# A Fourier-mixing and ELU kernel on one core: one gather for each backward tile instead of two, odd rows loaded in later steps, and scalar pairs in other steps

## Chip, cores and metric

The kernel runs on one core of one Trainium2 chip. The metric is the device time of one execution in microseconds (us). Given times are the median of the runs, with the lowest and highest; a profile comes from one execution of its own, whose time is given beside its span.

## What is computed

The reference takes `x` of shape 8 x 3008 x 256 in float32 and two weight matrices:

```
X = np.fft.fft(np.fft.fft(x, axis=1), axis=2).real      # 8 x 3008 x 256
h = X.reshape(24064, 256) @ w_in                         # w_in 256 x 2048
g = np.where(h > 0, h, np.exp(np.minimum(h, 0)) - 1)     # ELU
out = g @ w_out                                          # w_out 2048 x 256
```

## The kernel before, in words

**Main stream.** Only half of the frequencies along the sequence are computed; the other half follows by symmetry ("plus" and "minus" columns). The columns of all eight batches stand in rings in SBUF (`Rr`, `Ir`, `Rb`), and are worked through in 47 tiles of 256 columns. A tile has 8 slots, so there are 376 of them; a slot is called a step here. In each step TensorE (PE) does, in this order: `mm_P` (H from `Rr`), `mm_X1` of an earlier step (products of the second matrix), `mm_Q` (adds `Ir` to H), `mm_X2` and `mm_X3`. The second product is done with seven instead of eight block products (Winograd's scheme), which needs four sums of 128x256 blocks, `sum_1`, `sum_3`, `sum_2`, `sum_4`, on GpSimd (POOL). `mm_X1` uses the result of `sum_2` in its last product (the group pB<-G,WT). VectorE (DVE) has `even_part` (L1332, out E; it must have read H before `mm_Q` adds to it), `g_plus` and `g_minus` (L1362), `h_minus` (L1346). ScalarE (ACT) does the exponentials. At the end of each group of 8 steps DVE also combines and transposes a finished output tile (`comb_1`, `comb_2`, `comb_22`, `comb_3`, `turn_u`, `turn_v`), and SyncE (SP) issues the stores (L1563), 8 to 32 for each half of a tile.

**Side stream.** While the main stream works on one batch, the Fourier transform of the next is prepared in the gaps, for batches 2 to 7 by the "quarter" method. Four input tiles of up to 96 partitions with four rows of 256 values each are loaded by `load_quarter`, once for the near and once for the far part of the sequence. Two of the four tiles run forwards in memory and are loaded by SP (L337). The other two run backwards (j = 1, 2 in the near part, j = 0, 3 in the far part): two of their four rows come by an indirect DMA from POOL each (a gather, L303, with an index for each partition), the other two, called odd here, by SP with a negative step (L317, L326). Then POOL folds the tiles (`mirror_sum`, `channel_fold`), DVE adds halves (`half_sum`) and makes scalar pairs (`quarter_pairs` and `shift_pairs` with odd frequencies: two SCALAR_TENSOR_TENSOR of 94x128 in `turn`, L863), PE does small matmuls (QM), and DVE unfolds the result into the rings.

**What sets the order.** A list of events, each with a time in steps of `PERIOD` = 4.8, is sorted, and the functions are called in that order. Compute instructions and gathers are pinned to it on their engine (`pin`). DMAs of SP are not pinned: a scheduler places them in SP's queue, and each of them also waits for the transfer eight before it. For batch b the side stream's first step is r0 = 48b - 70 (`rel`). The near loads are events of steps 2 and 3 after r0, the far ones of steps 25 to 28, `mirror_sum` starts at steps 6 and 30, `shift_pairs` stands at steps 47 to 50, 54 and 55, always at the end of the step (4.25). `comb_1` and `comb_2` stand at 4.2 of every step that is 1 modulo 8, which steps 47 and 55 are.

Of the kernel before, what the change touches and what calls it, by code (L numbers as in the profile page):

```python
# [11 lines left out]
U32 = mybir.dt.uint32  # L12
# [5 lines left out]
SEQ = 3008  # L18
ND = 256
NDFF = 2048  # L20
NF = NDFF // 128
HALF = SEQ // 2
# [10 lines left out]
NP = 47  # L33
SHIFT = 8 * NP
# [141 lines left out]
def kernel(  # L176
# [7 lines left out]
    nc = tc.nc  # L184
    NB = x.shape[0]
# [20 lines left out]
    pin = tc.keep_in_program_order  # L206

    xt = x.tensor

    def xrows(b, row, step, n, rows=6):  # L210

        return bass.AP(
            tensor=xt,
            offset=x.offset + (b * SEQ + row) * ND,
            ap=[[step * ND, n], [1, rows * ND]],
        )


    xflat = x.rearrange("b s d -> (b s) d")
    ix = cpool.tile([128, 6], I32, tag="ix")  # L220
# [20 lines left out]
    def load_x(b):  # L241

        L = [
            spool.tile([128, 6 * ND], FP, tag=f"xl{j}", bufs=1, name=f"xl{j}")
# [3 lines left out]
        def back(j, few):  # L248
            cols = slice(0, 2 * ND) if few else slice(2 * ND, 6 * ND)
            c = 1 if few else 0  # L250
            pin(
                nc.gpsimd.indirect_dma_start(
                    out=L[j][:, cols],
                    out_offset=None,
                    in_=xflat,
                    in_offset=bass.IndirectOffsetOnAxis(
                        ap=ix[:, c : c + 1].bitcast(U32), axis=0
                    ),
                    element_offset=(b * SEQ + (HALF if j == 1 else 0)) * ND,
                )  # L260
            )
        def ahead(j, row):
            nc.sync.dma_start(out=L[j][:, 0 : 4 * ND], in_=xrows(b, row, 4, 128, 4))
            nc.sync.dma_start(
                out=L[j][:, 4 * ND :], in_=xrows(b, row + 512, 2, 128, 2)
            )

        loads = [lambda n=n: back(2 - n // 2, n % 2) for n in range(4)]
        return L, loads + [lambda: ahead(3, HALF), lambda: ahead(0, 0)]

# [18 lines left out]
    def load_quarter(b, j, far):  # L289

        L = spool.tile([128, 6 * ND], FP, tag=f"xl{j}", bufs=1, name=f"xq{j}")
        if j == 0:
            state["rest"] = L[:, 4 * ND :]
        state["L", j, far] = L = L[:, 0 : 4 * ND]
        rows = L.rearrange("p (m d) -> p m d", d=ND)
        back = j in (1, 2)
        base = b * SEQ + (0, SEQ, HALF, HALF)[j]
        if back != far:
            n = 94 if far else 96
            for i in (0, 2) if far else (3, 1):  # L300
                c = 3 if far else 5 if j == 1 and b == NB - 1 and i == 3 else 4
                pin(
                    nc.gpsimd.indirect_dma_start(  # L303
                        out=rows[0:n, i],
                        out_offset=None,
                        in_=xflat,
                        in_offset=bass.IndirectOffsetOnAxis(
                            ap=ix[0:n, c : c + 1].bitcast(U32), axis=0
                        ),
                        element_offset=(  # L310
                            b * SEQ + (HALF if j in (1, 3) else 0) + i
                        ) * ND,
                    )
                )
            row = base + (749 if far else -3)
            for i, shift in (((3, 0), (1, SHIFT)) if far else ((2, 0), (0, SHIFT))):
                nc.sync.dma_start(  # L317
                    out=rows[0 : 2 * NP, i],
                    in_=bass.AP(
                        tensor=xt,  # L320
                        offset=x.offset + (row - shift) * ND,
                        ap=[[2 * ND, 2], [-8 * ND, NP], [1, ND]],
                    ),
                )
            if not far:
                nc.sync.dma_start(  # L326
                    out=rows[2 * NP : 96, 0::2][:, 0:2],
                    in_=bass.AP(
                        tensor=xt,
                        offset=x.offset + (base - 752) * ND,  # L330
                        ap=[[2 * ND, 2], [ND, 2], [1, ND]],
                    ),
                )
            return

        def ahead(p, n, first, row, step):
            nc.sync.dma_start(  # L337
                out=rows[p : p + n, first::2][:, 0:2],
                in_=bass.AP(
                    tensor=xt,  # L340
                    offset=x.offset + row * ND,
                    ap=[[8 * ND, n], [step * ND, 2], [1, ND]],
                ),
            )

        for p, n in ((0, 80), (80, 14)) if far else ((0, 96),):
            ahead(p, n, int(far), base + 8 * p - 750 * far, 2)
        for p, m, n in ((0, 3, NP), (NP, 1, NP if far else 96 - NP)):
            ahead(p, n, int(not far), base + m - 752 * far, SHIFT)

    CC = cpool.tile([128, 384], FP, tag="CC")
    w2 = cpool.tile([128, NF * ND], FP, tag="w2")
# [245 lines left out]
    def act(o, i, func=AF.Copy, **kw):  # L598
        pin(nc.scalar.activation(out=o, in_=i, func=func, **kw))  # L599
# [226 lines left out]
    def quarter_row(b):  # L826

        L = state["L", 1, 0]
        act(L[0:1, 3 * ND :], state["L", 0, 0][0:1, 0:ND])

    def quarter_pairs(b, ri, kodd, m):
# [795 lines left out]
    state = {}  # L1627
# [27 lines left out]
    def at(t, fn):  # L1655
        events.append((t, len(events), fn))
# [69 lines left out]
    for slot in range(8):  # L1726
        i = slot % 2 * 8 + slot // 2
# [95 lines left out]
    for slot in range(total):  # L1823
        i = slot % 2 * 8 + slot // 2 if slot < 16 else slot
# [52 lines left out]
    def safe(col):  # L1877

        return 8 * ((col - 1 - RING) // TW) + 8 if col > RING else 0
# [39 lines left out]
    for n in range(16):  # L1919
        j, k = divmod(n, 4)  # L1920
# [23 lines left out]
    first = (6, 6, 7, 7, 7, 7, 7, 8, 8, 8, 9, 9, 9, 9, 12, 15)  # L1944
# [41 lines left out]
    for b in range(2, NB):  # L1986
        s0 = (b - 1) * steps_b
        r0 = 48 * b - 70

        def rel(step, dt, fn, *key):  # L1990
            at((r0 + step) * T + dt, lambda: fn(*key))

        for far, rows in (
            (0, ((0, 2, 0.2), (1, 2, 1.3), (3, 3, 0.2), (2, 5 if b == 2 else 3, 1.3))),
            (1, ((0, 27, 1.3), (1, 25, 0.2), (3, 28, 1.3), (2, 26, 3.0))),
        ):
            for j, n, dt in rows:
                rel(n, dt, load_quarter, b, j, far)
        rel(5, 3.0, quarter_row, b)
        for far, start in ((0, 6), (1, 30)):  # L2000
            for n in range(8):
                rel(start + n, 1.3, mirror_sum, (0, 3)[n % 2], far, (0, 2, 1, 3)[n // 2])
        for step, *key in (
            (13, 0, 0, 0), (20, 1, 0, 0), (21, 0, 0, 1), (22, 1, 0, 1),
            (35, 0, 1, 0), (36, 1, 1, 0), (37, 1, 1, 1), (38, 0, 1, 1),
        ):
            rel(step, 4.25, half_sum, *key)
        for step, *key in (
            (14, 0, 0, 0), (21, 1, 0, 0), (23, 0, 0, 1), (25, 1, 0, 1),
            (38, 0, 1, 0), (40, 1, 1, 0), (42, 1, 1, 1), (44, 0, 1, 1),  # L2010
        ):
            for ri in range(2):
                rel(step + ri, 1.3, channel_fold, ri, *key)
            kodd, far, h = key
            if h:
                rel(step, 4.0, channel_edge, kodd, far)
        for n in range(4):
            ri, m = divmod(n, 2)
            rel(46 + n, 1.3, quarter_pairs, b, ri, 0, 1 + m)
        for n, step in enumerate((43, 44, 45, 46, 51, 53)):  # L2020
            ri, m = divmod(n, 3)
            rel(step, 4.25, quarter_pairs, b, ri, 1, (2, 1, 3)[m])
        for step, *key in (
            (47, 0, 1, "u"), (48, 0, 0, "u"), (49, 0, 1, "v"), (50, 1, 0, "v"),
            (54, 1, 1, "u"), (55, 1, 1, "v"),
        ):
            rel(step, 4.25, shift_pairs, b, *key)
        for step, ri, kodd, finish, join in (
            (51, 0, 0, 0, 54),
            (56, 1, 0, 0, 59),  # L2030
            (59, 0, 1, 60, 75),
            (64, 1, 1, 66, 76),
        ):
            at_quarter(r0 + step, b, ri, kodd, r0 + finish, r0 + join)
        for kodd in range(2):
            step = s0 + (28, 38)[kodd]
            assert step >= safe(b * HALF + (kodd + 1) * RUN)
            at(step * T + 1.0, lambda b=b, kodd=kodd: spread_ext(b, kodd))
# [48 lines left out]
```

## Time and profile before

| what | value |
|---|---|
| median of 3 runs | 1941.01 us (1940.17 to 1946.64) |
| time of the profiled execution | 1948.1 us |
| its span, first to last instruction | 1946.3 us |
| granted TensorE clock | 0.999 |
| DVE busy | 1468.0 us (75%) |
| ACT busy | 876.5 us (45%) |
| POOL busy | 1380.8 us (71%) |
| mean of the 48 gathers on POOL (L303) | 1.21 us |
| SP transfers of the four tiles (L317, L326, L337) | 48, 12 and 84 |

A row of the page's groups gives line, engine, operation, out<-in and count, then busy time and mean of one, then the idle time of the engine just ahead of these instructions and what ended it. In the list of waits a row says which engine waited for which, with total us, number and longest. A row of the timeline gives start, length (both in us), engine, line, operation, tiles and count, and in brackets the idle time of the engine before it with its releaser. Matmuls are pipelined: their ends are modelled, and starts are the better measure.

### The profile page before, as it was taken

What the parts mean: (1) busy time and instruction counts of PE and PEld (TensorE: products, weight loads), DVE (VectorE), ACT (ScalarE), POOL (GpSimd) and SP (SyncE); (2) the same over time, 40 slices, a digit from 0 to 9 for tenths busy, and PEclk for the clock granted to TensorE, in tenths of its full rate; (3) what the DMA queues carried; (4) which work ended last, traced back from release to release, by engine and by line L of the source; (5) the groups of instructions that cost most, each with busy time, mean ns of one, the idle gap of its engine ahead of it and who ended that gap; (6) DMA issues with size and microseconds to landing.
All of it is one profiled execution on the core that took longest, in us unless ns stands there. A gap on an engine that the chain in (4) does not pass through costs nothing.

```text
span 1946.3 us, 27882 instructions
## 1 busy us (share of the span) xinstructions
PE 1909.4 (98%) x8972; PEld 1649.0 (85%) x8972; DVE 1468.0 (75%) x2786; ACT 876.5 (45%) x1709; POOL 1380.8 (71%) x1861
## 2 busy tenths in 40 slices
PE   9999999999999999999999999999999999999999
PEld 6888788888888888888888888888888888888887
DVE  8766667787778877788777887777877778767666
ACT  5754344444444444444444444444444444444443
POOL 4887668776687766777668776677766876556655
PEclk9999999999999999999999999999999999999999
DMA  8145211111011110111101111021110210100101
GB/s 333 44 33 29 64 24 42 48 25 32 12 43 36 27 34 12 44 34 29 29 19 44 31 29 27 12 52 38 26 22 12 51 20 17 17 12 12 22 12 23
DMA packets 278298, 71.50 MB, mean 37 GB/s; under 512 B 253574, under 2 KB 268170, under 8 KB 278152
## 3 DMA queue, kind: packets, MB, share of 16 engines
q1 hardware_dynamic: 268936, 61.58, 15.4%
q0 software_dynamic: 7040, 7.88, 1.4%
q8 instruction: 71, 1.16, 0.3%
q14 instruction: 75, 0.61, 0.1%
q10 hardware_dynamic: 2176, 0.26, 0.1%
HBM read 44.77 MB, written 24.80 MB: 36 GB/s over the span
## 4 chain that ended last, share of the span: by engine, by line
PE 86%; DVE 5%; POOL 4%; DMA 2%; issue 1%; SPq 1%; ACT 0%; DVEq 0%; POOLq 0%
PE H L587 34%; PE pB L587 15%; PE pC L587 15%; PE pD L587 15%; PE pA L587 8%; POOL G L596 2%; DMA x<-in_x_dram 2%; POOL xq L303 2%; DVE e L863 1%; DVE E L1332 1%; DVE v L593 1%; DVE G L1362 1%; DVE G L1346 0%; DVE u L593 0%; SPq L1162 0%
## 5 line engine op out<-in xcount | busy, mean ns | idle before, releaser
L596 POOL TENSOR_TENSOR G<-G 128x256 f32<-128x256 f32 x1440 | 1047.8, 737 | 497.5 <-DVE G L1362 344.0
L599 ACT ACTIVATE G<-H 128x512 f32<-128x512 f32 x376 | 224.5, 597 | 959.5 <-DVE G L1346 939.9
L1332 DVE SCALAR_TENSOR_TENSOR E<-Rb,wex,H 128x256 f32<-128x256 f32 x752 | 327.4, 476 | 356.6 <-PE H L587 351.6
L587 PE MATMUL H<-Ir,Wsc 128*128 128x256 f32 x1504 | 388.8, 381 | 12.3 <-DVE E L1332 12.2
L587 PE MATMUL H<-Rr,Wsc 128*128 128x256 f32 x1504 | 387.6, 380 | 0.5 <-ACT Wsc L599 0.5
L587 PE MATMUL pC<-G,WT 128*128 128x256 f32 x1440 | 369.6, 379 | 0.0
L587 PEld LDWEIGHTS H<-Ir,Wsc 128*128 128x128 f32 x1504 | 277.8, 189 | 65.2 <-DVE E L1332 21.2
L587 PEld LDWEIGHTS H<-Rr,Wsc 128*128 128x128 f32 x1504 | 282.1, 190 | 41.8 <-issue 1.7
L587 PEld LDWEIGHTS pC<-G,WT 128*128 128x128 f32 x1440 | 273.6, 190 | 37.2
L1346 DVE SCALAR_TENSOR_TENSOR G<-E,H 128x512 f32<-128x512 f32 x376 | 257.0, 683 | 58.6 <-POOL G L596 24.6
L1362 DVE SCALAR_TENSOR_TENSOR G<-G,H 128x512 f32<-128x512 f32 x376 | 255.8, 680 | 37.9 <-ACT G L599 37.5
L1362 DVE SCALAR_TENSOR_TENSOR G<-M,G 128x512 f32<-128x512 f32 x376 | 256.7, 683 | 0.8 <-ACT M L599 0.8
L599 ACT ACTIVATE G<-G 128x512 f32<-128x512 f32 x376 | 233.4, 621 | 0.0
L587 PE MATMUL pB<-G,w 128*128 128x256 f32 x784 | 229.3, 379 | 0.0
L587 PE MATMUL pA<-G,w 128*128 128x256 f32 x784 | 229.3, 379 | 0.0
L587 PE MATMUL pD<-G,w 128*128 128x256 f32 x784 | 229.3, 379 | 0.0
L587 PE MATMUL pB<-G,WT 128*128 128x256 f32 x720 | 215.7, 381 | 11.2 <-POOL G L596 11.2
L599 ACT ACTIVATE M<-G 128x512 f32<-128x512 f32 x376 | 223.9, 596 | 2.8 <-DVE G L1346 2.8
L599 ACT ACTIVATE M<-M 128x512 f32<-128x512 f32 x376 | 221.1, 588 | 0.1
L587 PE MATMUL pD<-G,WT 128*128 128x256 f32 x720 | 214.2, 379 | 0.0
L587 PEld LDWEIGHTS pA<-G,w 128*128 128x128 f32 x784 | 149.0, 190 | 20.5
L587 PEld LDWEIGHTS pB<-G,w 128*128 128x128 f32 x784 | 148.9, 190 | 20.4 <-PE H L587 0.2
(172 smaller groups left out, 1588.8 us busy)
## 6 DMA issues: line engine op xcount, KB each, us to landing
out_dram<-ot SPq DMA_DIRECT2D x496, 32.0 KB
xq<-in_x_dram SPq DMA_DIRECT2D x84, 94.0 KB
out_dram<-ot SPq DMA_DIRECT2D x256, 2.0 KB
Rb<-r SPq DMA_DIRECT2D x10, 376.0 KB
raw<-in_moe_w_in_dram SPq DMA_DIRECT2D x7, 512.0 KB
MC<-dft_mats SPq DMA_DIRECT2D x3, 943.5 KB
xq<-in_x_dram SPq DMA_DIRECT2D x12, 192.0 KB
xl<-in_x_dram SPq DMA_DIRECT2D x4, 512.0 KB
```

What stands on the lines that cost most here:

```text
L303: nc.gpsimd.indirect_dma_start(out=rows[0:n, i], out_offset=None, in_=xflat, in_offset=bass.IndirectOffsetOnAxis(ap=ix[0:n, c : c + 1].bit ...
L587: nc.tensor.matmul(out_, lhsT=lhsT, rhs=rhs, start=start, stop=stop, skip_group_check=True)
L593: pin(nc.vector.tensor_tensor(out=o, in0=a, in1=b, op=op))
L596: pin(nc.gpsimd.tensor_tensor(out=o, in0=a, in1=b, op=op))
L599: pin(nc.scalar.activation(out=o, in_=i, func=func, **kw))
L863: nc.vector.scalar_tensor_tensor(out=o, in0=a, scalar=twist_tab[0:94, c : c + 1], in1=b, op0=ALU.mult, op1=op,)
L1332: nc.vector.scalar_tensor_tensor(out=S.E[:, c], in0=Rb[:, cols(i)], scalar=wex[:, f : f + 1], in1=S.H[:, c], op0=ALU.mult, op1=ALU.add,)
L1346: nc.vector.scalar_tensor_tensor(out=two(S.G[:, 0:512])[:, :, ::-1], in0=two(S.E), scalar=2.0, in1=two(S.H), op0=ALU.mult, op1=ALU.subtract,)
L1362: nc.vector.scalar_tensor_tensor(out=o, in0=e, scalar=-1.0, in1=h, op0=ALU.add, op1=ALU.max)
```

## The change

1. `load_quarter` issues one gather for a backward tile, three adjoining rows long (96x768 or 94x768 values in place of two of 96x256 or 94x256). The middle one of the three is not a row that the tile needs there.
2. The odd rows are loaded by a new function, `load_odd`, called as events of later steps: 4 and 5 for the near part, 27 to 30 for the far part. One of the two odd rows of each backward tile lands on the middle row of the gather, so it must come after it.
3. The odd rows of the forward tiles are issued in cuts of 32 + 15 (or 48 + 1) partitions in place of 47 (or 49).
4. `quarter_row` moves from step 5 to step 4, and for the last batch copies one more row of one partition.
5. `shift_pairs` (0, 1, "u") moves from step 47 to 52, (1, 1, "v") from step 55 to 56.

In all, gathers go from 48 to 24, and SP transfers of the four tiles from 144 to 192.

```
         if back != far:
             n = 94 if far else 96
-            for i in (0, 2) if far else (3, 1):
-                c = 3 if far else 5 if j == 1 and b == NB - 1 and i == 3 else 4
...
+            i = 0 if far else 1
+            c = 3 if far else 5 if j == 1 and b == NB - 1 else 4
+            pin(
+                nc.gpsimd.indirect_dma_start(
+                    out=L[0:n, i * ND : (i + 3) * ND],
+                    out_offset=None,
+                    in_=xflat,
+                    in_offset=bass.IndirectOffsetOnAxis(
+                        ap=ix[0:n, c : c + 1].bitcast(U32), axis=0
+                    ),
+                    element_offset=(b * SEQ + (HALF if j in (1, 3) else 0) + i) * ND,
+                )
+            )
+            return
+        row = b * SEQ + (0, SEQ, HALF, HALF)[j] - 750 * far
+        for p, n in ((0, 80), (80, 14)) if far else ((0, 96),):
+            ahead(L, p, n, int(far), row + 8 * p, 2)
+    def load_odd(b, j, far):
+        L = state["L", j, far]
+        rows = L.rearrange("p (m d) -> p m d", d=ND)
+        base = b * SEQ + (0, SEQ, HALF, HALF)[j]
+        if (j in (1, 2)) != far:
             row = base + (749 if far else -3)
             for i, shift in (((3, 0), (1, SHIFT)) if far else ((2, 0), (0, SHIFT))):
                 nc.sync.dma_start(
...
-        for p, m, n in ((0, 3, NP), (NP, 1, NP if far else 96 - NP)):
-            ahead(p, n, int(not far), base + m - 752 * far, SHIFT)
+        for p, m, cuts in ((0, 3, (0, 32, NP)), (NP, 1, (0, 32, NP) if far else (0, 48, 49))):
+            for c, d in zip(cuts, cuts[1:]):
+                ahead(L, p + c, d - c, int(not far), base + m + 8 * c - 752 * far, SHIFT)
...
     def quarter_row(b):
         L = state["L", 1, 0]
+        if b == NB - 1:
+            act(L[0:1, ND : 2 * ND], L[0:1, 2 * ND : 3 * ND])
         act(L[0:1, 3 * ND :], state["L", 0, 0][0:1, 0:ND])
...
-        rel(5, 3.0, quarter_row, b)
+        for j, far, n, dt in (
+            (0, 0, 4, 0.2), (3, 0, 4, 1.3), (1, 0, 5, 0.2), (2, 0, 6 if b == 2 else 5, 3.1),
+            (1, 1, 27, 1.4), (2, 1, 28, 0.2), (0, 1, 29, 0.2), (3, 1, 30, 0.2),
+        ):
+            rel(n, dt, load_odd, b, j, far)
+        rel(4, 3.0, quarter_row, b)
...
-            (47, 0, 1, "u"), (48, 0, 0, "u"), (49, 0, 1, "v"), (50, 1, 0, "v"),
-            (54, 1, 1, "u"), (55, 1, 1, "v"),
+            (48, 0, 0, "u"), (49, 0, 1, "v"), (50, 1, 0, "v"), (52, 0, 1, "u"),
+            (54, 1, 1, "u"), (56, 1, 1, "v"),
         ):
             rel(step, 4.25, shift_pairs, b, *key)
```

More of the change, by code (lines that the diff above doesn't have):

```diff
@@ L294, in load_quarter, with ahead @@
         state["L", j, far] = L = L[:, 0 : 4 * ND]
-        rows = L.rearrange("p (m d) -> p m d", d=ND)
         back = j in (1, 2)
-        base = b * SEQ + (0, SEQ, HALF, HALF)[j]
         if back != far:
             n = 94 if far else 96
-            for i in (0, 2) if far else (3, 1):
-                c = 3 if far else 5 if j == 1 and b == NB - 1 and i == 3 else 4
[L302 to L313, printed above, removed]
-                )
+            i = 0 if far else 1
[9 more added lines that the diff above has]
+                    element_offset=(b * SEQ + (HALF if j in (1, 3) else 0) + i) * ND,
+                )
+            )
[3 more added lines that the diff above has]
+            ahead(L, p, n, int(far), row + 8 * p, 2)
+    def ahead(L, p, n, first, row, step):
+        nc.sync.dma_start(
+            out=L[p : p + n].rearrange("p (m d) -> p m d", d=ND)[:, first::2][:, 0:2],
+            in_=bass.AP(
+                tensor=xt,
+                offset=x.offset + row * ND,
+                ap=[[8 * ND, n], [step * ND, 2], [1, ND]],
+            ),
+        )
[4 more added lines that the diff above has]
+        if (j in (1, 2)) != far:
             row = base + (749 if far else -3)
@@ L334, in load_quarter @@
             return
[L336 to L347, printed above, removed]
-        for p, m, n in ((0, 3, NP), (NP, 1, NP if far else 96 - NP)):
-            ahead(p, n, int(not far), base + m - 752 * far, SHIFT)
+        for p, m, cuts in ((0, 3, (0, 32, NP)), (NP, 1, (0, 32, NP) if far else (0, 48, 49))):
+            for c, d in zip(cuts, cuts[1:]):
+                ahead(L, p + c, d - c, int(not far), base + m + 8 * c - 752 * far, SHIFT)
     CC = cpool.tile([128, 384], FP, tag="CC")
```

## The prediction

> **What bounds the kernel now.** First the page's busy row of PE and the list of PE's own waits:
>
> ```profile
> PE 1909.4 (98%) x8972; PEld 1649.0 (85%) x8972; DVE 1468.0 (75%) x2786; ACT 876.5 (45%) x1709; POOL 1380.8 (71%) x1861
> ```
> ```profile
> PE H L587 <- DVE E L1332: 12.2, 14, 1.2
> PE pB L587 <- POOL G L596: 11.2, 12, 1.5
> PE H L587 <- POOL xe L596: 5.3, 1, 5.3
> ```
>
> PE is the bound; what can be won is where it stands idle. Some 29 us do so under three names. By windows, the twelve waits for POOL lie in pairs, one pair in each of the six side streams; two of the fourteen for DVE (1.0 us) lie ahead of 300 us, the other twelve (11.2 us) again in pairs.
>
> The pair for POOL, in the timelines of POOL and PE of the far loads of batch 4:
>
> ```profile
> 800.19 3.03 POOL L596 TENSOR_TENSOR G<-G 128x256 f32<-128x256 f32 x4 [1.09 <-DVE G L1362]
> 803.40 1.50 POOL L303 DMA_INDIRECT xq<-in_x_dram,ix  x1 [0.18 <-issue]
> 805.21 1.49 POOL L303 DMA_INDIRECT xq<-in_x_dram,ix  x1 [0.30 <-issue]
> 806.73 3.34 POOL L596 TENSOR_TENSOR G<-G 128x256 f32<-128x256 f32 x4
> 810.25 1.49 POOL L303 DMA_INDIRECT xq<-in_x_dram,ix  x1 [0.18 <-DVE G L1362]
> 812.05 1.48 POOL L303 DMA_INDIRECT xq<-in_x_dram,ix  x1 [0.30 <-issue]
> 813.55 6.01 POOL L596 TENSOR_TENSOR G<-G 128x256 f32<-128x256 f32 x8
> ```
> ```profile
> 813.74 0.59 PE L587 MATMUL pB<-G,w 128*128 128x256 f32 x2
> 815.83 0.70 PE L587 MATMUL pB<-G,WT 128*128 128x256 f32 x2 [1.50 <-POOL G L596]
> 816.37 1.03 PE L587 MATMUL H<-Ir,Wsc 128*128 128x256 f32 x4
> ```
>
> Two gathers between two groups of sums make the second group late, and `sum_2` with it. Matmul starts stand 0.216 apart (22 to a step: 4.75 us), so 815.83 should have been 813.74 + 0.43 = 814.17: 1.66 late where the row says 1.50, and the next is 0.10 later still. A wait thus costs 0.26 more than its idle time.
>
> The waits for DVE, in the timeline of batch 5, step 47 and then step 52:
>
> ```profile
> 904.69 0.69 DVE L593 TENSOR_TENSOR v<-u,pC 128x512 f32<-128x512 f32 x1
> 905.30 1.83 DVE L863 SCALAR_TENSOR_TENSOR e<-o,twist_tab,e 94x128 f32<-94x128 f32 x2
> 907.05 0.86 DVE L1332 SCALAR_TENSOR_TENSOR E<-Rb,wex,H 128x256 f32<-128x256 f32 x2
> ...
> 930.03 0.68 DVE L1346 SCALAR_TENSOR_TENSOR G<-E,H 128x512 f32<-128x512 f32 x1
> 931.69 0.87 DVE L1332 SCALAR_TENSOR_TENSOR E<-Rb,wex,H 128x256 f32<-128x256 f32 x2 [0.98 <-PE H L587]
> ```
>
> In step 47 the scalar pair stands behind both `comb` operations, so E is late and PE waits 1.2. In step 52 DVE has 0.98 to spare ahead of the next E.
>
> [...] the pair's instruction takes from 0.35 to 1.23 us, 0.71 in the median. [...] here gathers do stand on POOL's row, among the sums. [...]
>
> **Part 1: 24 gathers go, 24 become longer.** The disputed price is the gather of three rows.
>
> ```profile
> L252 POOL DMA_INDIRECT xl<-in_x_dram,ix x8: 947/1091/1520, 1.7 to 63.8; - x8
> L303 POOL DMA_INDIRECT xq<-in_x_dram,ix x48: 920/1219/1510, 183.3 to 1534.0; - x48
> ```
>
> L252 gathers rows of 4 or 2 KB for 128 partitions, L303 rows of 1 KB for 94 or 96; both take 0.92 to 1.52 us. So the time doesn't go with bytes; I take 1.49, what the far ones take. Bounds: 0.92, and three times 1.49 = 4.47 (by bytes). In the far part, with one gather of length g: it runs from 803.40, sums may start at 803.45 + g = 804.94, just when DVE's next release is due (800.19 + 4.75 = 804.94). They end at 807.97, the second gather runs from 808.15 to 809.64, and the next release is due at 809.69. Nothing is late. Before, `sum_2` had a reserve of some 1.4: the first group was 1.79 late (806.73 - 804.94) and PE waited 0.42 at 809.32. Two gathers in succession make 2g - 2.98, so PE waits from g = 2.2 upwards. At 1.49 all twelve waits go: 11.2 + 12 x 0.26 = **14.3 us**. Near gathers (0.92) leave no wait on PE today, so their loss brings nothing.
>
> **Part 2: odd rows later.** SP issues 48 transfers more, at 0.34 to 0.62 each, most of them in stretches where it has nothing else: zero. The critical ones are the four that overwrite the gathers' middle rows. In SP's queue of the built program they stand, in each near part from batch 3, behind the 64 stores of a tile that crosses a boundary, where before they stood ahead. In the trace of before SP issues these stores from 434.03 on, and `mirror_sum` of row 1, the first to need the new rows, starts at 477.46:
>
> ```profile
> 434.03 31.74 SPq L1563 DMA_DIRECT2D out_dram<-ot  x64
> ...
> 477.46 0.90 POOL L596 TENSOR_TENSOR xq<-xq,xq 96x255 f32<-96x255 f32 x2
> ```
>
> The stores end at 465.8; four issues of some 0.62 end at 468.3. Each waits for the one eight before it, and 64 in 31.74 us means some 4 us to land: ready at 470 to 472, 5 to 7 us before use. Both instants follow the main stream, so this holds when it is faster. Should the cover go, POOL would stand in `mirror_sum` with all its sums behind it, and PE after these: one us for each us late, in six near parts. The gathers' own landing (2.8 to 6.5 us) ends long before SP is free. Far: 20 stores stand ahead similarly, with about 5 us spare (stores end 826.7, six issues and 4 us to land, use at 838.6). The first `mirror_sum` of each part uses rows that stay where they were. Behind SP's moved transfers are only the loads of `Rb` (and, once, the row that these read), made many steps ahead. `quarter_row` on ACT now waits for its gather, issued two steps (9.5 us) before it: zero; if late, ACT's exponentials queue behind it.
>
> **Part 3: scalar pairs.** Both waits per batch leave: 11.2 + 12 x 0.26 = 14.3, and the small lag of step 54, whose pair stays, lies outside these twelve. What comes back: in step 52 DVE is free from 930.63 (next operation's start after h) until E at 931.69: 1.06. A pair takes 1.3 to 1.75 from start to start in this trace when POOL's sums run beside it, as they do here (929.66 to 932.70). E may be about 0.15 late without cost (its end at 932.56 against `mm_Q` at 932.78). Worst: 1.75 - 1.06 - 0.15 + 0.1 = 0.64 a batch. The nearest case is step 54, where a pair follows the joins of the ring in just the same way, and there PE loses 0.2 to 0.3 with 0.13 less room. I take 0.2: 6 x 0.2 = **1.2**. Bounds 0 and 3.8. Step 56: with no lag from step 55, h would end by 950.7 and a pair at 1.5 by 952.2, when E is due at 952.1; that step has `mm_X3` between P and Q (0.86 of room): zero. Net gain **13.1**.
>
> **Part 4: the front.** PE waits 5.3 once for POOL xe, which waits for xs. A 2-row, a 94-row and a 47-row transfer leave SP's queue ahead of the last xs, but xe_dr there waits for its data until 188.78 anyway; larger gathers run beside. I take 1.0 (from -1 to +4).
>
> Sum: 14.3 + 13.1 + 1.0 = 28.4. On the profiled execution, 1948.1 (span 1946.3): 1919.7. That one is 7.1 above the median of the runs; the losses are fixed stalls, so from 1941.0 I get **1912.6**.
>
> **Rivals.**
> A, forecast: 1912.6, its own range 1908 to 1918. Chance 0.70.
> B, slower: a gather's time goes with its bytes. [...] Against: L252. At 4.47 the first far group is 2.96 late and the second 4.5 late against a PE that has already lost 1.5: waits of 1.5 and 3.1, with 0.26 for each 5.1 a batch, 30.6 us for 14.3; near gathers at 3 x 0.92 = 2.77 are 2 x 2.77 - 2.98 = 2.56 late, above the reserve by 1.2, so 6 to 7 more: 1941.0 + 16.3 + 6.5 - 14.1 = 1949.7. It decides from g = 2.2; from about 4.2 it has eaten the rest. Chance 0.07.
> C: step 52 becomes what step 47 was, 1.45 a batch: 8.7 in place of 1.2, so 1920. For: the unfold stands there. Chance 0.10.
> D: odd rows land late, 13 us after the stores' end and not 6: 2 us in six parts, 1925. Chance 0.08.
> The pieces cancel or do nothing (1941): 0.05.
>
> **How the numbers follow.** A, C and D make faster 0.88, of which 0.01 goes to slower for a wait not foreseen: 0.87; slower is B with that, 0.08; same 0.05. Under 0.3% (5.8 us) a measurement can't be told from no change. Range: 1906 (A with 4 in the front and no new stall, and 2 us of scatter) to 1927 (gather as long as today's two, POOL's gain gone: 1912.6 + 14.3), which holds A, C and D.
>
> **What would show it.** PE's waits for POOL G at pB gone; those for DVE E reduced to some 2 us; L303 at 24 with a mean of 1.2; a wait of POOL xq for a DMA would speak for D, of PE for DVE in step 52 for C. I am wrong if the gather's mean exceeds 2.2 or POOL waits for xq.

## The result and the profile after

The changed kernel takes 1912.98 us (median of 4 runs, 1911.92 to 1914.55) against 1942.34 for the one before in the same set (4 runs, 1940.17 to 1946.64): ratio 0.9847, 95% interval 0.9827 to 0.9866. The forecast was 1912.6 us, faster. In a later set, with more runs of the kernel before, the medians are 1912.37 and 1939.74, a ratio of 0.9855 (0.984 to 0.987). The profiled execution of the changed kernel took 1911.92, its span is 1910.1.

The page's busy row and the head of PE's own list of waits for the changed kernel (the helper of PE is now L592, of POOL L601, `even_part` L1339, the gathers L301):

```profile
PE 1901.3 (100%) x8972; PEld 1648.8 (86%) x8972; DVE 1466.7 (77%) x2786; ACT 876.9 (46%) x1710; POOL 1352.6 (71%) x1837
```
```profile
PE H L592 <- ACT Wsc L604: 1.2, 2, 0.6
PE M L592 <- DVE zero L579: 1.1, 1, 1.1
PE H L592 <- DVE mid L1616: 1.1, 1, 1.1
PE H L592 <- DVE E L1339: 1.0, 2, 0.7
```

All three names that led the list before are gone from its head: no wait of PE for POOL G at pB is left, the fourteen for DVE E are two (1.0 us, both ahead of 300 us), and the one for POOL xe isn't there. What remains lies in the first 215 us and the last four, apart from lags that are too short for this list.

The row of the gathers among POOL's groups, then POOL's timeline in the far loads of batch 4, the place that the prediction worked through, and PE's timeline behind the second gather:

```profile
L301 POOL DMA_INDIRECT xq<-in_x_dram,ix x24 | 29.2, 1215 | 3.9 <-issue 2.7
```
```profile
782.35 3.03 POOL L601 TENSOR_TENSOR G<-G 128x256 f32<-128x256 f32 x4 [1.08 <-DVE G L1369]
785.57 1.50 POOL L301 DMA_INDIRECT xq<-in_x_dram,ix  x1 [0.18 <-issue]
787.11 3.40 POOL L601 TENSOR_TENSOR G<-G 128x256 f32<-128x256 f32 x4
790.70 1.50 POOL L301 DMA_INDIRECT xq<-in_x_dram,ix  x1 [0.18 <-issue]
792.22 3.41 POOL L601 TENSOR_TENSOR G<-G 128x256 f32<-128x256 f32 x4
```
```profile
795.21 0.59 PE L592 MATMUL pB<-G,w 128*128 128x256 f32 x2
795.64 0.59 PE L592 MATMUL pB<-G,WT 128*128 128x256 f32 x2
796.08 1.03 PE L592 MATMUL H<-Ir,Wsc 128*128 128x256 f32 x4
```

The gather of three rows takes 1.50 us here, as the gather of one row did. The sums behind the first one start at 787.11; they were due at 782.35 + 4.75 = 787.10. Those behind the second start at 792.22, 0.37 after their due time of 791.85, and that is inside the reserve of 1.4: the matmul that uses `sum_2` starts at 795.64, 0.43 behind its neighbour at 795.21, which is two starts of 0.216 and no wait.

Step 52 of batch 5, into which a scalar pair was moved, in the timelines of DVE and PE:

```profile
908.18 0.68 DVE L1353 SCALAR_TENSOR_TENSOR G<-E,H 128x512 f32<-128x512 f32 x1
908.78 1.40 DVE L870 SCALAR_TENSOR_TENSOR e<-o,twist_tab,e 94x128 f32<-94x128 f32 x2
910.11 0.86 DVE L1339 SCALAR_TENSOR_TENSOR E<-Rb,wex,H 128x256 f32<-128x256 f32 x2
```
```profile
910.50 0.59 PE L592 MATMUL pB<-G,WT 128*128 128x256 f32 x2
911.02 1.13 PE L592 MATMUL H<-Ir,Wsc 128*128 128x256 f32 x4
```

The pair takes 1.33 from its start to that of E. `mm_Q` starts at 911.02, where 910.50 + 0.43 = 910.93 would have been without delay: 0.09 late, and one of its matmuls loses 0.10 more. That is the lag of 0.2 per batch that was forecast, and too short to be listed as a wait.

### The profile page after: what moved, and what is told of

Its sections match the earlier page's. It is cut to its first block, busy times and chain, and to the rows that moved or that the text cites. A ratio compares the mean times of both kernels' runs of the same rounds, so it can differ in the third digit from the quotient of the medians.

```text
span 1910.1 us, 27916 instructions
## 1 busy us (share of the span) xinstructions
PE 1901.3 (100%) x8972; PEld 1648.8 (86%) x8972; DVE 1466.7 (77%) x2786; ACT 876.9 (46%) x1710; POOL 1352.6 (71%) x1837
## 4 chain that ended last, share of the span: by engine, by line
PE 96%; DVE 2%; DMA 0%; issue 0%; ACT 0%; POOL 0%; POOLq 0%; DVEq 0%
PE H L592 38%; PE pB L592 17%; PE pC L592 17%; PE pD L592 17%; PE pA L592 9%; DMA xl<-in_x_dram,ix 0%; DVE E L1339 0%; DVE e L689 0%; DVE o L689 0%; POOL w L601 0%; DVE G L1369 0%; DVE e L870 0%; DVE G L1353 0%; DVE Rr L598 0%; DVE pow L460 0%
## 5 line engine op out<-in xcount | busy, mean ns | idle before, releaser
L601 POOL TENSOR_TENSOR G<-G 128x256 f32<-128x256 f32 x1440 | 1049.3, 738 | 505.5 <-DVE G L1369 349.8
L1339 DVE SCALAR_TENSOR_TENSOR E<-Rb,wex,H 128x256 f32<-128x256 f32 x752 | 327.5, 476 | 337.3 <-PE H L592 331.4
L592 PE MATMUL H<-Ir,Wsc 128*128 128x256 f32 x1504 | 388.1, 380 | 1.1 <-DVE E L1339 1.0
L592 PE MATMUL H<-Rr,Wsc 128*128 128x256 f32 x1504 | 387.6, 380 | 0.5 <-ACT Wsc L604 0.5
L592 PE MATMUL pC<-G,WT 128*128 128x256 f32 x1440 | 369.5, 379 | 0.0
L592 PEld LDWEIGHTS H<-Ir,Wsc 128*128 128x128 f32 x1504 | 277.7, 189 | 52.1 <-DVE E L1339 7.5
L592 PEld LDWEIGHTS H<-Rr,Wsc 128*128 128x128 f32 x1504 | 282.1, 190 | 41.6 <-issue 2.3
L592 PEld LDWEIGHTS pC<-G,WT 128*128 128x128 f32 x1440 | 273.6, 190 | 37.2
L592 PE MATMUL pB<-G,w 128*128 128x256 f32 x784 | 229.3, 379 | 0.0
L592 PE MATMUL pA<-G,w 128*128 128x256 f32 x784 | 229.3, 379 | 0.0
L592 PE MATMUL pD<-G,w 128*128 128x256 f32 x784 | 229.2, 379 | 0.0
L592 PE MATMUL pB<-G,WT 128*128 128x256 f32 x720 | 214.4, 379 | 0.0
L592 PE MATMUL pD<-G,WT 128*128 128x256 f32 x720 | 214.1, 379 | 0.0
L592 PEld LDWEIGHTS pA<-G,w 128*128 128x128 f32 x784 | 148.9, 190 | 20.5
L592 PEld LDWEIGHTS pB<-G,w 128*128 128x128 f32 x784 | 148.9, 190 | 20.4 <-PE H L592 0.2
```

The lines of the kernel that those rows point to most:

```text
L592: nc.tensor.matmul(out_, lhsT=lhsT, rhs=rhs, start=start, stop=stop, skip_group_check=True)
L601: pin(nc.gpsimd.tensor_tensor(out=o, in0=a, in1=b, op=op))
L1339: nc.vector.scalar_tensor_tensor(out=S.E[:, c], in0=Rb[:, cols(i)], scalar=wex[:, f : f + 1], in1=S.H[:, c], op0=ALU.mult, op1=ALU.add,)
```

## The experiments

**The pairs alone.** The kernel before with one edit:

```
-            (47, 0, 1, "u"), (48, 0, 0, "u"), (49, 0, 1, "v"), (50, 1, 0, "v"),
-            (54, 1, 1, "u"), (55, 1, 1, "v"),
+            (48, 0, 0, "u"), (49, 0, 1, "v"), (50, 1, 0, "v"), (52, 0, 1, "u"),
+            (54, 1, 1, "u"), (56, 1, 1, "v"),
```

> The kernel before with the scalar pairs in the new steps, nothing else. Additive theory (gathers, pairs and the front are three separate gains): 13 us less than before, about 1929; PE's waits for DVE E fall from 14 (12.2 us) to 2 (1.0 us), the twelve for POOL G at pB (11.2 us) and the one for POOL xe (5.3 us) stay. Rival 1 (step 52 becomes what step 47 was): within 4 us of before, with waits for DVE E in step 52. Rival 2 (the pairs carry nearly the whole gain, since PE's waits for POOL follow from its waits for DVE): about 1915, and the waits for POOL go too.

Measured: 1926.41 (6 runs) against 1939.89 (19 runs), ratio 0.9927 (0.9911 to 0.9942), 13.5 us less. PE's list of waits in its profile:

```profile
PE pB L587 <- POOL G L596: 11.2, 12, 1.5
...
PE H L587 <- DVE E L1332: 1.0, 2, 0.7
```

The twelve waits for POOL are untouched and those for DVE have gone. Both rivals fall. The wait for POOL xe, which should have stayed, isn't in the list though the front of this kernel is that of before.

**The gathers without the pairs.** The changed kernel with the list of `shift_pairs` as before, the edit above turned round.

> The changed kernel with the scalar pairs back in steps 47 and 55, so single gathers, later odd rows and cuts remain. Additive theory: 14.3 us from the gathers and 1 to 5 from the front, so 1922 to 1927; PE's twelve waits for POOL G gone, fourteen for DVE E (12 us) there. Rival (the gains are not separate, PE's gain at the gathers is lost again at the waits for DVE or the stores): 1935 or more.

Measured: 1925.44 (6 runs), ratio 0.9923 (0.9907 to 0.9939), 14.45 us less than before. PE's list is the mirror image of the last one, with no row for POOL G:

```profile
PE H L592 <- DVE E L1339: 12.4, 15, 1.2
```

The gain is at the low end of what was expected, 14.3 and nothing from the front.

**Two gathers again.** The changed kernel with a loop of two gathers of one row each in `load_quarter` (and without the extra row copied in `quarter_row`); odd rows, cuts and pairs as changed:

```
-            i = 0 if far else 1
-            c = 3 if far else 5 if j == 1 and b == NB - 1 else 4
...
-                    out=L[0:n, i * ND : (i + 3) * ND],
+            for i in (0, 2) if far else (3, 1):
+                c = 3 if far else 5 if j == 1 and b == NB - 1 and i == 3 else 4
...
+                        out=L[0:n, i * ND : (i + 1) * ND],
```

> The changed kernel with two gathers of one row each again for a backward tile; later odd rows, cuts and pairs stay as changed. If the number of gathers is the whole cause of PE's waits for POOL: twelve waits of some 11 us come back and the time is 14 us above the changed kernel, about 1927. Rival (the later odd transfers, which left the stretch in which the gathers run, removed part of these waits): under 8 us above it, with waits for POOL G below 6 us.

Measured: 1926.12 (6 runs), 13.75 above the 1912.37 that the changed kernel has in another set (the kernel before has 1939.89 in this one and 1939.74 in that), and the waits for POOL are back:

```profile
PE pB L594 <- POOL G L603: 11.1, 12, 1.5
```

Taken from start to start in the trace, these twelve matmuls come 13.1 us late and the ones behind them 0.10 each, 1.2 in all: 14.3. So the second gather of a tile brings back the whole loss. It does so in the far parts alone, where a gather takes 1.5 us: the near parts have two gathers again as well, at 0.92, and none of the twelve waits. The later odd transfers and the cuts, which this kernel has, remove nothing: it is within 0.3 us of the pairs alone.

**The cuts alone.** The kernel before with

```
-        for p, m, n in ((0, 3, NP), (NP, 1, NP if far else 96 - NP)):
-            ahead(p, n, int(not far), base + m - 752 * far, SHIFT)
+        for p, m, cuts in ((0, 3, (0, 32, NP)), (NP, 1, (0, 32, NP) if far else (0, 48, 49))):
+            for c, d in zip(cuts, cuts[1:]):
+                ahead(p + c, d - c, int(not far), base + m + 8 * c - 752 * far, SHIFT)
```

> The kernel before with the odd rows of forward tiles cut 32 + 15 (32 + 15 or 48 + 1) in place of 47 (47 or 49), nothing else. Front theory F1 (a transfer of 47 partitions [...] held back the last xs): PE's wait for POOL xe falls from 5.3 to under 1 us, and the time by about 5, to 1937. F2 (it is the transfers that no longer stand ahead of xs in SP's queue): the wait stays near 5 or grows with the two extra transfers, 1942 to 1944. F3 (the wait varies from run to run): between these, and the same kernel before shows another value in a second profile.

Measured: 1939.81 (14 runs), ratio 0.9996 (0.9988 to 1.0004). PE's wait for POOL xe isn't in its profile either. The time speaks against F1, the missing wait against F2; what is left is F3, that the wait belongs to one execution.

**The kernel before, profiled again.** No edit.

> The kernel before, profiled a second time. If the wait of PE for POOL xe (5.3 us) belongs to this kernel, it is there again and the span is near 1946. If it belongs to one execution (no profile of the kernels with the front unchanged has shown it so far), it is under 0.5 us and the span is near 1938, 1.8 under the median of 1939.9.

This execution took 1939.9, with a span of 1938.1. The head of PE's list:

```profile
PE H L587 <- DVE E L1332: 12.6, 15, 1.2
PE pB L587 <- POOL G L596: 11.2, 12, 1.5
PE H L587 <- ACT Wsc L599: 1.2, 2, 0.6
```

The two regular stalls are there to 0.4 us, the wait for POOL xe is gone. It belongs to the first profile's execution, which took 8 us longer. Of the 41 executions of the kernel before that these sets hold, five take 1945 to 1948.3 and the rest 1939 to 1944; the changed versions scatter upwards too (two gathers up to 1930.3, pairs alone up to 1929.3). Only one of the five was profiled, so whether the others have this wait, and what causes it, stays open.

**The changed kernel again, and two versions of it, in one set.** First without an edit.

> The changed kernel once more, beside the kernel before on the same chip. Additive theory: the two parts run alone gave 13.5 and 14.45 us against 1939.9; together 28.0, so 1911.9 and a ratio of 0.9856. Rival (they share some of the gain): 1915 or more.

Measured: 1912.37 (4 runs) against 1939.74 (9 runs), ratio 0.9855 (0.984 to 0.987): 27.4 us less. The parts alone sum to 13.5 + 14.45 = 27.9. They add up within 0.6, which is less than the runs scatter.

**The pairs moved further.**

```
-            (48, 0, 0, "u"), (49, 0, 1, "v"), (50, 1, 0, "v"), (52, 0, 1, "u"),
-            (54, 1, 1, "u"), (56, 1, 1, "v"),
+            (48, 0, 0, "u"), (49, 0, 1, "v"), (50, 1, 0, "v"), (58, 0, 1, "u"),
+            (61, 1, 1, "u"), (56, 1, 1, "v"),
```

> The changed kernel with two scalar pairs moved on, from step 52 to 58 and from 54 to 61, where PE has small matmuls of the side stream between its two products. Theory (the small lags that are left in steps 52 and 54, 0.18 and 0.2 to 0.3 us a batch, come from these pairs): 2.3 to 2.9 us less than the changed kernel over six batches. Rival (steps 58 and 61 have no more room than these, since the unfold and the joins stand there): the same within 1 us, with new lags there, or slower by up to 8.

Measured: 1909.78 (5 runs), ratio to the kernel before 0.9842 (0.9829 to 0.9856), 2.6 us under the changed kernel. In its trace the lags of steps 52 and 54, which the changed kernel has in all six batches, are gone and steps 58 and 61 have none: in step 58 DVE waits another 1.03 to 1.05 us for PE between the pair and the next E. It is the fastest version here. The intervals of the two ratios overlap, so the 2.6 rest on the trace and on the medians (the fastest run of the changed kernel, 1911.92, lies above all runs of this one, of which the slowest took 1911.73).

**The odd rows at once.** `load_odd` is called right behind `load_quarter` and the later events are gone. In the last batch `quarter_row` then copies after the odd row has come, so that one row of one partition holds a neighbouring input row.

```
                 rel(n, dt, load_quarter, b, j, far)
+                rel(n, dt + 0.001, load_odd, b, j, far)
```

> The changed kernel with the odd rows called right behind the gathers and not some steps further on. If the later steps matter (SP stands in the wait for a gather with stores and forward rows behind it): 3 to 10 us slower than the changed kernel, with a wait of POOL or ACT for stores or rows. If the place doesn't matter, since SP has nothing due behind it: within 2 us of the changed kernel.

Measured: 1914.69 (4 runs), ratio 0.9868 (0.9853 to 0.9883), 2.3 us above the changed kernel. From start to start PE loses just these 2.3 us in one place (1.41 + 0.47 + 0.39 at 1388 to 1392), and ACT's timeline shows whence:

```profile
1377.12 0.59 ACT L604 ACTIVATE M<-M 128x512 f32<-128x512 f32 x1
1385.36 0.72 ACT L604 ACTIVATE xq<-xq 1x256 f32<-1x256 f32 x2 [7.65 <-DMA xq<-in_x_dram]
1385.98 0.57 ACT L604 ACTIVATE G<-H 128x512 f32<-128x512 f32 x1
```

In the last batch `quarter_row` touches a row that an odd transfer writes, so ACT waits for that transfer; it stands in SP's queue behind 32 stores (1365.76 to 1381.31), and the exponentials of a step queue behind ACT's wait. In the other five batches the early place costs nothing. So neither expectation fits as a whole: the wait is of the kind that the first one named, ACT's for a row behind stores, but it comes in one batch only, and the loss is below the 3 us given there.

**Other shapes of gather.** Near gathers fetch four rows, far ones have 96 indices in place of 94 (the added ones fill rows of two partitions that nobody reads; the index table's base and the offset move by 16 rows for it):

```
             n = 94 if far else 96
-            i = 0 if far else 1
+            n = 96
+            i = 0
+            m = 3 if far else 4
...
-                    out=L[0:n, i * ND : (i + 3) * ND],
+                    out=L[0:n, 0 : m * ND],
```

> The changed kernel with gathers of other shapes: the near ones fetch four rows (4 KB, 96 indices) in place of three, the far ones three rows with 96 indices in place of 94. If a gather's time on POOL goes with bytes: near 0.93 x 4/3 = 1.24 us, far 1.5. If it goes with the number of indices and 94 is a dear one: near 0.93 and far 0.93 us. The time of the kernel stays that of the changed one within 2 us in both cases, since no gather keeps PE waiting.

Measured: 1912.32 (4 runs), the changed kernel's time. The row of the gathers and the last line of their detail, for this kernel:

```profile
L303 POOL DMA_INDIRECT xq<-in_x_dram,ix x24: 917/925/959, 182.6 to 1499.1; - x24
...
DMA to landing us min/median/max: 3.3/3.9/4.4
```

and for the changed kernel, in its second profile:

```profile
L301 POOL DMA_INDIRECT xq<-in_x_dram,ix x24: 926/1228/1504, 183.6 to 1500.2; - x24
...
DMA to landing us min/median/max: 3.4/6.6/10.2
```

Neither three nor four rows cost more than one, which took 0.92 to 0.96 us with 96 indices in the near parts of the kernel before. What made the far gathers dear was the 94 (1.50): with 96 indices all take 0.92 to 0.96 us. This points to a smaller edit that no run here tests. Two gathers of one row with 96 indices would hold POOL for about 2.15 us (0.92 + 0.30 + 0.92, an estimate from the near parts, where PE doesn't wait), and the prediction's working has PE wait from 2.2 upwards: padding the far gathers of the kernel before to 96 might have removed most of the twelve waits too.

**Three gathers.** The kernel with two gathers, with `(0, 1, 2) if far else (3, 2, 1)` in its loop: the price that rival B put on POOL.

> The changed kernel with the three rows of a backward tile fetched by three gathers of one row: the price that the rival with time by bytes put on POOL, 4.5 us far and 2.8 near for a tile. That rival's working: 30.6 us of waits in the far parts and 6 to 7 in the near ones, so 37 us above the changed kernel, 1950. If PE's reserve ahead of sum_2 is larger than the 1.4 us taken, or the main stream swallows part: 1935 to 1945, with PE waits for POOL G of 20 to 28 us.

Measured: 1957.21 (4 runs), ratio 1.0086 (1.0066 to 1.0105): 44.8 us above the changed kernel and slower than before. PE waits for POOL G 31.9 us in 23 places, so the second expectation fails, and the first, 37, is short by 8. The missing part is in PE's timeline, far part of batch 6:

```profile
1304.36 0.70 PE L594 MATMUL pB<-G,WT 128*128 128x256 f32 x2 [3.28 <-POOL G L603]
1304.89 1.48 PE L594 MATMUL H<-Ir,Wsc 128*128 128x256 f32 x4
1306.17 1.91 PE L594 MATMUL pC<-G,WT 128*128 128x256 f32 x4
```

Four matmuls of pC take 1.70 from start to start (1306.17 to 1307.87) where they take 0.86 elsewhere. The granted clock of 1305 to 1311 is 0.72. Eight matmuls at 0.43 in place of 0.216 cost 1.7 us; that happens in five of the six far parts. In three of them it follows the first wait, and the second is then 1.60 in place of 3.27 to 3.29, so the slow matmuls only fill what PE would have waited anyway. In two it follows the second wait and adds 1.7 each, 3.4 in all.

The rest of the missing 8 lies in the waits themselves. Without slow matmuls a far part costs 5.7 (2.06 and 3.43 late, 0.10 behind each) for B's 5.1: three gathers with 0.30 between them hold POOL for 5.1 us, and B's one gather was to take 4.5. Six parts at 5.7 are 34.2 for 30.6, the near ones cost 7.6 and 1.1 behind them for 6 to 7, and with the clock's 3.4 the sum is 46.3, 1.5 above what was measured.

## Why the prediction was right

**What bounds the kernel** held: two stalls that recur in each of the six side streams, each of them 11 to 12 us idle and 0.26 more for each wait. Taking one away doesn't move the other.

**Part 1 (14.3).** Right in mechanism and size: 13.75 by the kernel with two gathers, 14.45 by the one without the new pairs, and 14.3 when the twelve waits are summed in the trace. The disputed price of 1.49 was measured as 1.50, and the sums behind the second gather, computed to be just in time, were 0.37 late within their reserve. The near gathers' loss brought nothing, as said. Inferring from L252 that time doesn't go with bytes was right, but the reason for 0.92 against 1.5 was not seen then: it is the number of indices, 96 or 94 (the far gathers too take 0.92 to 0.96 with 96).

**Part 2 (zero).** Right. POOL waits for no transfer of the tiles: its list of waits in the changed kernel names no DMA. In the near part of batch 3 the stores end at 453.3, the four odd transfers are issued by 456.5, and the row is used at 464.21, in the timelines of SP (stores and last odd transfer) and POOL:

```profile
421.69 31.62 SPq L1570 DMA_DIRECT2D out_dram<-ot  x64
...
455.86 0.64 SPq L343 DMA_DIRECT2D xq<-in_x_dram  x1
```
```profile
464.21 0.89 POOL L601 TENSOR_TENSOR xq<-xq,xq 96x255 f32<-96x255 f32 x2
```

That is 7.7 us from issue to use, for 9.2 in the forecast. The order behind the gathers doesn't need the later steps: with the odd rows at once five batches lose nothing, and the 2.3 us in the last come from `quarter_row`, which there has to wait for an odd row. The risk was named with the right engine, since ACT's exponentials do queue behind a late `quarter_row`, but only where it touches the rows in question.

**Part 3 (13.1).** Right: 13.5 alone on the kernel before, and 1925.44 - 1912.37 = 13.1 on top of the gathers. The term for the new lag in step 52, 1.2, measures 0.18 x 6 = 1.1 (0.08 and 0.10 in each batch). Rival C, which puts 8.7 there, falls.

**Part 4 (1.0), and the level from which the sum was subtracted.** This is the step that was wrong. PE's wait of 5.3 for POOL xe was read as a property of the kernel, of which a part might go. A second profile doesn't have it, and the pairs alone, which keep the front of before, don't have it either. The term is zero for the median. The text said that the profiled execution was 7.1 above the median, and then, in the next half sentence, that "the losses are fixed stalls"; these 7.1 were mostly that wait. PE's timeline in the first profile and in the second:

```profile
197.96 3.74 PE L587 MATMUL H<-MC,xe 128*8 128x189 f32 x24 [5.28 <-POOL xe L596]
```
```profile
191.46 2.09 PE L587 MATMUL H<-MC,xe 128*8 128x189 f32 x24
```

The wait cost 5.3, and the 24 matmuls behind it took 3.74 at a granted clock of 0.61 (198 to 202), where in the second profile they take 2.09: 1.65 more. The difference of the two first profiles, 1946.3 - 1910.1 = 36.2, is therefore no measure of the change; with the second profiles it is 1938.1 - 1911.9 = 26.2 (that of the changed kernel took 1913.68, above its median), and by the medians 27.4, which is 14.3 + 13.1.

That the forecast still stood 0.4 from the result is in part luck: 1.0 too much gain was taken from a median of three runs, 1941.0, that lies 1.1 to 1.3 above that of larger sets (1939.89, 1939.74).

**The rivals.** B's path from a longer hold of POOL to PE is real, as three gathers show, which end slower than before. Its premise fails, because a longer row cost no time on POOL here (1.50 for one row and for three with 94 indices, 0.92 to 0.96 for one, three and four with 96). The three gathers cost more than its sum because of the gaps between them and of the slow matmuls, a term that it lacked. D fell with Part 2.

## What to carry to other kernels

Where one engine is busy 98% of the time and waits in the same places of every batch, sum these waits from start to start, with the slower start behind each (0.10 here). The two gains here added up within 0.6 us (13.5 and 14.45 alone, 27.4 together), and each could be tested alone. A wait that occurs once, in a profile that stands above the median, is checked in a second profile before it enters the sum. A small operation that can't be avoided goes into a step in which other work of the bound engine stands ahead of the deadline: the pairs lost their last 2.6 us only there.

## What was not expected of the hardware

**Indices, not bytes.** A gather of the tiles from POOL took 0.92 to 0.96 us with 96 indices, for rows of 1, 3 or 4 KB, and 1.48 to 1.56 with 94, mostly 1.50. The eight gathers of 128 indices at the kernel's start (L252) took 0.94 to 1.52, and the longest are not the same ones in each execution (the last took 1.52 in the first profile of the kernel before and 0.99 in that of the changed kernel), so there something else adds to the time. The landing goes the same way: the two far gathers between 786 and 800 us land after 9.3 us with 94 indices and after 3.4 with 96, with 787 packets in that queue against 128. Of the 787 packets 644 have 8 bytes, 322 for each gather; with 96 indices there are none of these. In the packet records of the changed kernel's first profile, the first gather of a far part (94 indices), while it is alone, has 1.9 to 2.0 of its 6 KB packets under way at a time and at most 3; a near gather (96 indices) has 8.6 to 10.6, at most 16 to 19. That POOL's own time is longer with 94 indices is shown, and so is the difference in packets; the cause of neither is.

**Matmuls at half rate behind a wait.** In the kernel with three gathers PE runs eight matmuls at half rate (0.43 us from start to start in place of 0.216) after waits of 3.28 and 3.29 us, and in three parts already after one of 1.87 to 1.90; in one part neither a wait of 1.90 nor one of 3.27 is followed by them. No wait for POOL G of up to 1.6 us in the kernels here is followed by such a run; in the first profile of the kernel before, the granted clock is 1.00 in the stretches with these twelve waits. The wait of 5.28 in that profile ends at 197.96, and the granted clock is 0.50 from 197.8 to 201.0 and 1.00 again from 201.2. In both kernels the slow stretch lasts some 3.4 us: eight matmuls at 0.43 in one, 3.41 of a clock of 0.5 in the record of the other. The length of the wait alone doesn't decide: the slow matmuls came after 1.87 to 1.90 in three of six parts, and in one they did not come after 3.27. What decides is not shown.
